# A long convolution and a state-space layer on one core: real and imaginary rows interleaved, the exchange in two strided transfers, a new order

## The chip, the cores and the metric

The kernel runs on one core of one Trainium2 chip. The metric is the device time of an execution in microseconds (us). A core has five engines, each with its own instruction queue: TensorE (PE in the profile, with weight loads shown as PEld), VectorE (DVE), ScalarE (ACT), GpSimd (POOL) and SyncE (SP). In this kernel SP and POOL mostly issue DMA transfers, which 16 DMA engines carry out.

## The reference

Two layers are computed over sequences of 2048 steps and 1024 channels in bf16, and their outputs are put side by side.

```python
# A: shifted key times value, long convolution by FFT, gate
for t in range(ks):
    k_shift = k_shift + k_pad[:, t:t + S, :] * shift_k[:, ks - 1 - t]
kv = k_shift * v
y = irfft(rfft(kv, 2 * S) * rfft(ssm_k, 2 * S))[:S]      # length 4096
A = q * (y + kv * ssm_D)
# B: diagonal complex recurrence
Lam_bar = exp(exp(log_dt) * Lam)
Bu = einsum("bld,pd->blp", x, ((Lam_bar - 1) / Lam)[:, None] * Bmat)
for t in range(L):
    h = Lam_bar * h + Bu[:, t]
B = 2 * einsum("blp,dp->bld", h, Cmat).real + x * Dskip
out = concatenate([A, B], axis=-1)
```

## The kernel before

The whole program is one text, `ORDER`, of some 1500 words. Each word names a task and its arguments; after a colon it names the buffers that the task takes: units of a shared SBUF arena of 53 units of 1024 bf16 columns (a), PSUM banks (p, eight), buffers of the recurrence (h, three) and buffers for transform weights (w, three). The words are executed in order at build time, and every engine's queue receives its instructions in that order; semaphores make an instruction wait for its operands and for the last readers of the buffer it overwrites. `ORDER` therefore sets both the order on each engine and which older buffer each task has to wait for. No planner stands behind it.

**The recurrence (B)** goes in 16 chunks of 128 steps. For a chunk the input is loaded transposed (x), then come four U tasks of two halves each (TensorE, 16 matmuls a half, L435), the copies out of PSUM (ue, ScalarE, L437), a product with a rotation table and a sum (r1 and r2, VectorE, L450 and L457), the carry (cy, ScalarE, L459), two scans (sc, VectorE, L463), a second product and sum (r3, r4, L450 and L469), the output matmuls (y, TensorE, four tasks of four matmuls L479 and one matmul for the skip term L482 for each half of the channels), the copy (ye, L488) and the store (yst, POOL, L490).

**The convolution (A)** does a transform of length 4096 in two stages, 128 by 32. Stage 1 makes kv on VectorE (L514 to L529), transforms it and the filter (am L534, hm L572), copies (ae L540, he L578) and stores to the DRAM tensors Ys_kv and Ys_h (ast L543, hst L581). Stage 2 is the part that the change edits. It runs over 16 pairs of groups. For pair i:

- lw.i loads the pair's transform weights into one of three wslots (SP, L585), lh.i and lk.i load the two stage-1 results (SP, L590);
- sh and sk, one each per group (group 2i and 2i+1), do the 32-point transforms of filter and kv: four matmuls each (L602) whose weights lie in columns 0 to 63 of the group's part of the wslot;
- she copies the filter's spectrum from PSUM to half t=0 of the tile hab, ske that of kv to x16 (ScalarE, L612 and L620);
- sw.i fills half t=1 of hab with the same rows, real and imaginary rows exchanged (POOL issues SBUF-to-SBUF transfers, L625);
- pr.i multiplies both halves of hab by x16 (VectorE, L631), which gives all four real products of a complex one;
- sa, one per group, sums them and transforms back: eight matmuls (L643) with the two remaining blocks of weights;
- sae copies (ScalarE, L651) and vst stores to the DRAM tensor Vs (POOL, L654).

Stage 3 loads Vs (vl, L659), transforms (a3, L671), copies (a3e, L678), multiplies by q (qm, VectorE, L680) and stores (ost, POOL).

A wslot is free for the next pair's lw when the last sa of the pair that used it has read it. The pairs do not run in the order of their numbers; in this `ORDER` lw goes 3, 1, 0, 2, 4, 5, 6, 8, 7, 9, 11, 10, 15, 12, 14, 13.

The 128 partitions of hab hold four runs of 32 rows: real parts of one half of the channels, imaginary parts of that half, and the same for the other half of the channels. sw.i.q for q from 0 to 3 therefore moves one run of 32 rows to its neighbour's place:

```python
o = q ^ 1
dma(hab[32*q:32*q+32, 1], hab[32*o:32*o+32, 0])
```

Of the kernel before, what the change touches and what calls it, by code (L numbers as in the profile page):

```python
# [28 lines left out]
WC = 352  # L29
# [3 lines left out]
def a_constants():  # L33
# [39 lines left out]
bl.1.0:a46 bT.1.0:p1 sin2 bc.1.0 x.1:a47 x.0:a26 ld_F U.1.0.0:a24p4 U.1.3.0:p5 bl.2.0:a48 kvb.2:a49 kp.-2 bc.2.1 bc.7.1 kvm.0:a8 bc.3.0 bl.5.1:a50
vp.1:a40 eo stt kva.0 bl.4.1:a51 kvc.2 bl.5.0:a42 U.0.0.0:a44p7 U.0.0.1 kvb.0:a43 U.1.0.1 bT.2.0:p6 U.0.3.0:p1 ue.0.0 U.0.3.1 bc.2.0 gz bl.4.0:a46
U.1.3.1 bT.4.1:p2 bT.5.1:p3 bT.5.0:p0 cl.3.0:a48 bT.4.0:p7 U.0.1.0:p6 ue.0.3 bc.4.1 bc.4.0 bc.5.1 U.0.1.1 bc.5.0 U.1.1.0:p1 z1 U.0.2.0:p2 U.0.2.1
ue.0.2 ue.0.1 r1.0:a36 U.1.2.0:p7 kvc.3 r2.0:h0 vp.0:a32 kvc.1 kvc.0 cl.2.1:a34 sc.0.1 sc.0.0 cT.2.1:p3 cc.2.1 x.2:a35 z2 cl.1.1:a51 cl.3.1:a50
hl.2:a28 cl.1.0:a42 U.1.2.1 U.2.0.0:a30p0 U.2.0.1 ue.2.0 U.2.1.0:p2 U.2.1.1 ue.2.1 cT.1.1:p6 cc.1.1 U.1.1.1 ue.1.0 ue.1.1 ue.1.2 ue.1.3 r1.1:a8
cT.1.0:p3 r3.0:a0 cc.1.0 r2.1:h1 cT.3.0:p0 cc.3.0 x.3:a46 r4.0 cx.4.1 am.0.1:p2p6 ae.0.1.1:a44 ae.0.0.1 cx.7.0 cl.0.1:a34 am.1.0:p4p1 ae.1.1.0:a40
U.2.3.0:p7 ae.1.0.0 U.2.3.1 ue.2.3 ld_sd:a51 am.0.0:p5p3 ae.0.0.0 U.3.0.0:a32p0 hl.0:a4 U.3.2.0:p6 ae.0.1.0 U.3.0.1 ue.3.0 am.1.1:p2p1 U.2.2.0:p4
hl.3:a6 ae.1.0.1 hl.1:a36 hT.0.0:p7 hc.0.0:a48 hd.0 cy.1 sc.1.0 sc.1.1 ae.1.1.1 U.2.2.1 ue.2.2 r1.2:a8 r3.1:a0 cT.3.1:p5 hT.0.3:p3 cc.3.1 r2.2:h2 r4.1  # L80
# [666 lines left out]
```

## Time and profile before

| | us |
|---|---|
| device time, median of 3 runs | 374.81 |
| the three runs | 372.85, 374.81, 376.28 |
| the profiled execution | 376.32 |
| span of the profiled execution | 374.5 |
| PE busy | 339.6 (91%) |
| PEld busy | 227.5 (61%) |
| DVE busy | 316.8 (85%) |
| ACT busy | 282.6 (75%) |
| POOL busy | 97.7 (26%) |

The granted TensorE clock is 0.983 of full speed on average. The transfers move 101.14 MB at a mean of 270 GB/s; 58.47 MB are issued on the hardware queue (SP) and 42.09 MB on the software queue (POOL).

A share of busy time is a mean over stages that have different limits. The head (weights, tables, first chunks), the middle with stage 1 and the recurrence, the part with stage 2 and the tail have to be read one by one. In a group's row, "idle before" is time in which the engine waited ahead of that instruction, and the name behind it is what ended most of that wait. A line number is that of the printed code.

### The profile page before, as it was taken

Reading aid. Unit: us, or ns where it says so; the run is one execution under the profiler, and the core shown is the slowest. Engines: PE = TensorE matmul, PEld = TensorE weight load, DVE = VectorE, ACT = ScalarE, POOL = GpSimd, SP = SyncE. Lnnn points to the kernel's source line nnn. Section 1 sums busy time; section 2 is a strip of 40 time slices with the busy share of each in tenths; the row PEclk is TensorE's granted clock in tenths of the full one; section 3 lists DMA queues with packets and bytes.
Section 4 is the critical chain, followed back from the end, with each engine's and each line's share of the span. In section 5 each row is a group of like instructions: output and inputs, shape, how many; then the busy total and the mean of one; then the engine's idle time right before and its main releaser. Section 6 shows DMA issues by size and latency. Waiting matters only on the chain.

```text
span 374.5 us, 9087 instructions
## 1 busy us (share of the span) xinstructions
PE 339.6 (91%) x3721; PEld 227.5 (61%) x3721; DVE 316.8 (85%) x249; ACT 282.6 (75%) x538; POOL 97.7 (26%) x167
## 2 busy tenths in 40 slices
PE   4597999999999999999988999697979969999990
PEld 1597997546768895665554495263745746665440
DVE  5998999999999999999969793988764767985970
ACT  4899987946769999986666689696979967327570
POOL 5000000313232232450430415251532431200231
PEclk9999999999999999999998999999999989999996
DMA  6999999486896999998799899989997999798973
GB/s 194 328 313 266 274 333 148 125 297 151 264 314 245 248 315 242 280 284 329 228 290 294 294 218 239 355 256 296 308 270 240 276 313 301 273 329 283 349 302 137
DMA packets 61989, 101.14 MB, mean 270 GB/s; under 512 B 29902, under 2 KB 31966, under 8 KB 61948
## 3 DMA queue, kind: packets, MB, share of 16 engines
q1 hardware_dynamic: 49148, 58.47, 55.7%
q0 software_dynamic: 12800, 42.09, 34.2%
q8 instruction: 29, 0.48, 0.5%
q14 instruction: 12, 0.10, 0.1%
HBM read 52.31 MB, written 33.55 MB: 229 GB/s over the span
## 4 chain that ended last, share of the span: by engine, by line
PE 65%; DMA 14%; ACT 7%; DVE 5%; issue 4%; POOL 2%; POOLq 0%; DVEq 0%; ACTq 0%
PE bank L479 22%; PE bank L435 22%; DMA wslot<-a_c_W 9%; DMA arena<-arena 4%; PE bank L643 4%; PE bank L534 4%; PE bank L572 4%; PE bank L671 3%; PE bank L602 3%; PE bank L556 2%; ACT BT L411 2%; DVE arena L514 2%; ACT arena L612 1%; PE bank L482 1%; DVE arena L631 1%
## 5 line engine op out<-in xcount | busy, mean ns | idle before, releaser
L435 PEld LDWEIGHTS <-BT 128*128 128x128 bf16 x2048 | 118.2, 98 | 14.8 <-issue 6.5
L435 PE MATMUL bank<-arena,BT 128*128 128x128 bf16 x2048 | 125.4, 220 | 1.2 <-ACT BT L411 0.7
L479 PE MATMUL bank<-CT,gslot 128*128 128x512 bf16 x512 | 123.5, 379 | 0.4 <-ACT arena L612 0.2
L479 PEld LDWEIGHTS <-gslot 128*128 128x128 bf16 x512 | 45.6, 98 | 50.5 <-issue 5.4
L463 DVE TENSOR_TENSOR_SCAN gslot<-rtab,gslot 128x1040 bf16<-128x1040 f32 x32 | 73.1, 2312 | 1.8 <-ACT gslot L459 1.5
L631 DVE TENSOR_TENSOR arena<-arena 128x4096 bf16<-128x4096 bf16 x16 | 36.6, 2290 | 24.1 <-DMA arena<-arena 20.7
L625 POOL DMA_DIRECT2D arena<-arena x64 | 31.4, 497 | 62.8 <-ACT arena L612 36.0
L450 DVE TENSOR_TENSOR arena<-arena,Z 128x4096 bf16<-128x4096 bf16 x16 | 36.5, 2284 | 12.6 <-ACT arena L437 12.6
L437 ACT CAST arena<-bank 128x512 bf16<-128x512 f32 x64 | 39.5, 640 | 10.0 <-PE bank L435 6.9
L540 ACT CAST arena<-bank 128x512 bf16<-128x512 f32 x64 | 36.9, 649 | 7.1 <-PE bank L534 6.8
L612 ACT CAST arena<-bank 128x512 bf16<-128x512 f32 x64 | 34.3, 633 | 8.4 <-PE bank L602 8.4
L578 ACT CAST arena<-bank 128x512 bf16<-128x512 f32 x64 | 36.4, 694 | 4.5 <-PE bank L572 2.3
L620 ACT CAST arena<-bank 128x512 bf16<-128x512 f32 x64 | 36.4, 661 | 2.8 <-PE bank L602 2.8
L651 ACT CAST arena<-bank 128x512 bf16<-128x512 f32 x64 | 35.0, 652 | 4.2 <-PE bank L643 3.9
L450 DVE TENSOR_TENSOR arena<-gslot,Z 128x4096 bf16<-128x4096 bf16 x16 | 36.6, 2289 | 0.7
L581 POOL DMA_DIRECT2D Ys_h<-arena x32 | 23.0, 724 | 49.5 <-ACT arena L578 45.1
L488 ACT CAST arena<-bank 128x512 bf16<-128x512 f32 x32 | 19.1, 609 | 19.7 <-PE bank L482 15.6
L514 DVE TENSOR_TENSOR arena<-arena 128x4096 bf16<-128x4096 bf16 (+3 forms) x16 | 30.0, 1883 | 0.5 <-ACT arena L388 0.5
L678 ACT CAST arena<-bank 128x512 bf16<-128x512 f32 x32 | 17.1, 612 | 17.6 <-PE bank L671 17.6
L602 PE MATMUL bank<-arena,wslot 64*64 64x512 bf16 x256 | 20.7, 402 | 9.0 <-DMA wslot<-a_c_W 9.0
L482 PE MATMUL bank<-Dd,arena 128*128 128x128 bf16 x128 | 28.0, 219 | 0.0
L643 PE MATMUL bank<-arena,wslot 64*64 64x512 bf16 x256 | 18.3, 409 | 5.5 <-DVE arena L631 5.3
(96 smaller groups left out, 374.0 us busy)
## 6 DMA issues: line engine op xcount, KB each, us to landing
Ys_kv<-arena POOLq DMA_DIRECT2D x16, 512.0 KB, 5.3
Ys_h<-arena POOLq DMA_DIRECT2D x32, 256.0 KB, 3.8
arena<-Ys_h SPq DMA_DIRECT2D x16, 512.0 KB, 7.8
arena<-Ys_kv SPq DMA_DIRECT2D x16, 512.0 KB, 7.3
arena<-arena POOLq DMA_DIRECT2D x64, 128.0 KB, 6.6
Vs<-arena POOLq DMA_DIRECT2D x16, 512.0 KB, 5.6
arena<-Vs SPq DMA_DIRECT2D x16, 512.0 KB, 8.9
arena<-in_A_k_dram SPq DMA_DIRECT2D x8, 512.0 KB, 5.6
```

Source lines behind the costliest of these rows:

```text
L435: nc.tensor.matmul(pu[:, w, jl, :], BT[:, 2 * jp + jl, w, d, :], xT[:, d, :], start=(d == 0), stop=(d == ND - 1))
L437: E["ue"] = lambda i, jp: nc.scalar.copy(st["u", i][:, :, 2 * jp:2 * jp + 2, :], st.pop(("pu", i, jp)))
L450: nc.vector.tensor_mul(m, s_, win(Z))
L463: nc.vector.tensor_tensor_scan(gf, rtab[:].rearrange("p j t -> p (j t)"), gf, 0.0, ALU.mult, ALU.add)
L479: nc.tensor.matmul(py, h[:, w, j, 2:GW], CT[:, j, w, dh * 512:(dh + 1) * 512], start=(j == 0 and w == 0), stop=False)
L514: nc.vector.tensor_mul(m[:, 0:h0, :], kring_[:, s0:s0 + h0, :], wbc_[:, 0:h0, :])
L540: nc.scalar.copy(st["ysb", n2][:, p, dh * 512:(dh + 1) * 512], st.pop(("pa", n2, p, dh)))
L578: nc.scalar.copy(st["yh", hf, s][:, p, e, :], st.pop(("pb", hf, s, e, p)))
L612: nc.scalar.copy(st["hab", i][:, t, a, l, :], st.pop(("ps", nm, g, l)))
L620: nc.scalar.copy(st["x16", i][:, a, l, :], st.pop(("ps", "k", g, l)))
L631: nc.vector.tensor_mul(hab, st.pop(("x16", i)).rearrange("p a l d -> p (a l d)").unsqueeze(1).to_broadcast([P, 2, 2 * D]), hab)
L651: nc.scalar.copy(st["vsb", i][:, a, dh * 512:(dh + 1) * 512], st.pop(("pv", g, dh)))
```

## The change

The rows of the 32-point transform are ordered anew: instead of 32 real rows and then 32 imaginary rows, real and imaginary rows alternate. This takes a transposition of the constant weights, in the forward blocks and in the two backward blocks that read the product. The exchange of real and imaginary rows is then one of even and odd partitions, so one transfer moves all 64 even rows of the 128 partitions to the odd ones, and a second does the reverse. Per pair there are two issues of 64 rows (256 KB each) where there were four of 32 (128 KB each): 32 issues in all for 64. Each row's data is as long as before.

Each group's weights also lose 32 columns (64 to 95) that no task of the order read, so a pair's load falls from 176 to 160 KB.

`ORDER` is wholly new: nearly every word stands at another place and takes other buffers. Except for the exchange, each kind of task occurs as often as before. In stage 2, lw keeps its order of pairs.

```diff
-WC = 352
+WC = 320
...
-            W[l, :, g, 0:64] = fw.reshape(64, 64)
-            W[l, :, g, 64:96] = fw[:, :, 0, :].reshape(64, 32)
+            W[l, :, g, 0:64] = fw.transpose(0, 1, 3, 2).reshape(64, 64)
...
-                W[dh, :, g, 96 + 128 * l:160 + 128 * l] = wa.reshape(64, 64)
-                W[dh, :, g, 160 + 128 * l:224 + 128 * l] = wb.reshape(64, 64)
+                W[dh, :, g, 64 + 128 * l:128 + 128 * l] = wa.transpose(1, 0, 2, 3).reshape(64, 64)
+                W[dh, :, g, 128 + 128 * l:192 + 128 * l] = wb.transpose(1, 0, 2, 3).reshape(64, 64)
...
-lw.9:w2 sh.18:p2p7 sw.7.1 sh.19:p6p4 sw.7.0 sa.17:p1p3
+lw.9:w2 sh.19:p2p1 yst.8 ske.15.0 lh.11:a20 ye.10.1:a27 sae.16.0:a50
...
     def swap(dma, i, q):
-        o = q ^ 1
-        dma(st["hab", i][32 * q:32 * q + 32, 1, :, :, :], st["hab", i][32 * o:32 * o + 32, 0, :, :, :])
+        dma(st["hab", i][q:P:2, 1, :, :, :], st["hab", i][1 - q:P:2, 0, :, :, :])
...
-                    c0 = a * WC + 96 + 128 * l + 64 * t
+                    c0 = a * WC + 64 + 128 * l + 64 * t
```

Line numbers of the code after the change are three to seven lower than those of before. The next rows show the order of instructions on an engine, with line, operation, output and input, and in brackets the semaphores waited for: DMASW and DMAHW count landings of transfers issued by POOL and by SP, eight counters each; the others count an engine's instructions.

On POOL, one pair's exchange (pair 9) between two stores of Vs, before:

```order
L625 DMA arena<-arena 32x2048 [waits DVE_49,DMASW1_49,PE_49,Activation_49]
L625 DMA arena<-arena 32x2048 [waits DMASW2_49,PE_49]
L625 DMA arena<-arena 32x2048 [waits DMASW3_49]
L625 DMA arena<-arena 32x2048 [waits DMASW4_49]
L654 DMA Vs<-arena 128x2x1024 [waits DMAHW2_49,DMASW5_49,Activation_49]
```

An exchange after, with the stores of Vs around it:

```order
L647 DMA Vs<-arena 128x2x1024 [waits DMAHW0_49,DMASW4_49,Activation_49]
L618 DMA arena<-arena 64x2048 [waits DVE_49,DMASW5_49,PE_49,Activation_49]
L618 DMA arena<-arena 64x2048 [waits DMASW6_49]
L647 DMA Vs<-arena 128x2x1024 [waits DMASW7_49]
L647 DMA Vs<-arena 128x2x1024 [waits DMASW0_49,Activation_49]
```

Four issues have become two. Each of POOL's issues still waits for the landing counter of the one eight issues before it.

On ScalarE, the copies ahead of the first copy (L612, after L607) that belongs to pair 9, whose first sh stands behind the reload of a wslot that pair 6 used. Before:

```order
376 L651 CAST arena_91<-bank7_99 128x512
377 L651 CAST arena_91<-bank6_98 128x512
378 L620 CAST arena_91<-bank4_96 128x512
379 L620 CAST arena_91<-bank1_93 128x512
380 L620 CAST arena_91<-bank3_95 128x512
381 L620 CAST arena_91<-bank0_92 128x512
382 L488 CAST arena_91<-bank5_97 128x512
383 L612 CAST arena_91<-bank7_99 128x512
```

After:

```order
374 L644 CAST arena_91<-bank4_96 128x512
375 L614 CAST arena_91<-bank0_92 128x512
376 L614 CAST arena_91<-bank6_98 128x512
377 L614 CAST arena_91<-bank3_95 128x512
378 L614 CAST arena_91<-bank5_97 128x512
379 L614 CAST arena_91<-bank2_94 128x512
380 L434 CAST arena_91<-bank1_93 128x2x256
381 L614 CAST arena_91<-bank7_99 128x512
382 L485 CAST arena_91<-bank4_96 128x512
383 L644 CAST arena_91<-bank0_92 128x512
384 L607 CAST arena_91<-bank7_99 128x512
```

Between the last copy of pair 6's back transform (the first row of the second piece) and the first copy of pair 9 there now also stand two more copies of kv's spectrum (L614), one of a U task (L434) and one of pair 8's back transform (L644), so the TensorE work that they read lies inside this reload too.

On VectorE, the products (L631, after L624) of the last three pairs, 12, 14 and 13, with the first product of chunk 13 (L450, after L447, with the table Z1). Before:

```order
214 L631 TENSOR_TENSOR arena_91<-arena_91 128x4096 [waits DMASW6_49,DMASW1_49,DMASW7_49,DMASW0_49,Activation_49]
215 L450 TENSOR_TENSOR arena_91<-arena_91,Z1_74 128x4096 [waits DMAHW6_49,Activation_49]
216 L631 TENSOR_TENSOR arena_91<-arena_91 128x4096 [waits DMASW5_49,DMASW4_49,DMAHW0_49,DMASW3_49,DMAHW3_49,DMASW2_49,Activation_49]
217 L457 TENSOR_TENSOR gslot0_85<-arena_91 128x16x128 [waits DVE_49]
218 L631 TENSOR_TENSOR arena_91<-arena_91 128x4096 [waits DMASW2_49,DMASW7_49,DMASW1_49,DMAHW2_49,DMASW0_49,Activation_49]
219 L463 SCALAR_TENSOR_TENSOR gslot0_85<-rtab_76,gslot0_85 128x1040 [waits DVE_49,Activation_49]
```

After:

```order
211 L624 TENSOR_TENSOR arena_91<-arena_91 128x4096 [waits DMASW6_49,DMAHW7_49,DMASW5_49,Activation_49]
212 L624 TENSOR_TENSOR arena_91<-arena_91 128x4096 [waits DMASW1_49,DMASW0_49,Activation_49]
213 L624 TENSOR_TENSOR arena_91<-arena_91 128x4096 [waits DMAHW1_49,DMAHW2_49,DMASW3_49,DMAHW4_49,DMASW2_49,Activation_49]
214 L447 TENSOR_TENSOR arena_91<-arena_91,Z1_74 128x4096 [waits DMAHW3_49,PE_49]
215 L454 TENSOR_TENSOR gslot0_85<-arena_91 128x16x128 [waits DVE_49]
216 L460 SCALAR_TENSOR_TENSOR gslot0_85<-rtab_76,gslot0_85 128x1040 [waits DVE_49,Activation_49]
```

The first product and sum of chunk 13, which stood between the last three pairs' products, now stand behind them. In the same place on TensorE the U tasks of the last two chunks stand ahead of the remaining y tasks of chunk 12.

More of the change, by code (lines that the diff above doesn't have):

```diff
@@ L73 @@
[L73 to L80, printed above, removed]
@@ new lines @@
+U.3.3.0:p4 he.0.0.0.1 he.0.0.0.0 hc.0.5:a20 U.3.3.1 cT.2.1:p7 hc.0.2:a36 cc.2.1 ae.0.1.1 ast.0 cx.6.1 vp.2:a24 U.3.2.0:p0 hm.0.5.1:p6p2 U.3.2.1
+he.0.5.1.0:a28 he.0.5.1.1 cx.5.0 ue.3.2 cy.2 sc.2.1 sc.2.0 kvb.4:a27 kva.6 r3.2:a0 kvb.6:a40 r4.2 y.0.0.0:p1 y.0.0.1 ue.3.3 hm.0.2.0:p7p3 hT.0.3:p6
+hc.0.3:a52 r1.3:a16 y.0.0.2 y.0.0.3 ye.0.0:a21 hm.0.5.0:p2p0 kvc.4 he.0.5.0.0 he.0.5.0.1 hT.0.4:p4 hc.0.4:a20 he.0.2.0.1:a38 y.1.0.0:p6 hm.0.2.1:p1p2
+y.1.0.1 he.0.2.0.0 he.0.2.1.0 hst.0.2.0 hT.0.1:p0 hc.0.6:a36 hT.0.7:p4 hm.0.4.1:p3p7 he.0.4.1.1:a22 cx.4.1 y.1.0.2 y.1.0.3 ye.1.0:a30 he.0.4.1.0
@@ new lines @@
+am.2.0:p1p5 ae.2.0.0:a32 cx.5.1 hst.0.0.0 cx.7.0 hst.0.5.1 y.1.1.0:p7 y.1.1.1 y.1.1.2 hm.0.6.1:p6p3 hc.0.7:a31 am.2.1:p1p4 ae.2.0.1 ae.2.1.1 y.1.1.3
+r2.3:h1 kvm.5:a0 kp.4 ye.1.1 he.0.2.1.1 kvm.9:a16 kva.5 kva.9 kvb.5:a41 ae.2.1.0 cy.3 sc.3.0 kvb.9:a47 sc.3.1 vp.3:a34 kvm.8:a0 r3.3:a16 ld_G
+he.0.6.1.1:a50 kva.8 r4.3 he.0.6.1.0 kvc.6 y.0.1.0:p1 kvb.8:a16 y.0.1.1 ast.1 kvc.5 kvm.7:a0 hc.0.1:a42 hst.0.0.1 vp.4:a44 kvc.8 x.4:a43 kva.7
+kvb.7:a17 hm.0.4.0:p4p7 y.0.1.2 y.0.1.3 ye.0.1 kvc.9 y.2.0.0:p2 hst.0.2.1 y.2.0.1 y.2.0.2 y.2.1.0:p5 y.2.1.1 he.0.4.0.0 y.2.1.2 am.4.0:p3p6
@@ new lines @@
+ae.4.0.0:a38 ae.4.1.0 y.2.1.3 am.4.1:p0p1 ye.2.1:a20 ae.4.0.1 hm.0.6.0:p4p3 he.0.6.0.0 ae.4.1.1 y.2.0.3 ast.2 ye.2.0 yst.1 hm.0.7.1:p6p5
+he.0.7.1.1:a32 he.0.4.0.1 hst.0.6.0 hm.0.7.0:p0p4 yst.0 he.0.7.0.0 hst.0.5.0 U.4.0.0:a36p1 he.0.6.0.1 he.0.7.1.0 hst.0.7.0 he.0.7.0.1 U.4.0.1
+am.3.0:p2p5 ae.3.0.0:a30 U.4.1.0:p7 U.4.2.0:p0 U.4.3.0:p3 U.4.1.1 ue.4.1 ue.4.0 U.4.3.1 U.4.2.1 kp.5 ue.4.3 ae.3.1.0 ue.4.2 r1.4:a0 r2.4:h0 lw.3:w0
+kvc.7 kvm.11:a0 kva.11 kvb.11:a48 am.3.1:p6p4 ae.3.1.1 x.5:a27 U.5.0.0:a28p2 U.5.3.0:p7 U.5.3.1 ae.3.0.1 U.5.1.0:p1 kvm.10:a0 U.5.0.1 kva.10
@@ new lines @@
+ast.3 kp.6 hl.6:a30 hT.1.0:p1 hc.1.0:a16 hd.1 r3.4:a0 vp.5:a40 kvc.11 r4.4 kvc.10 ast.5 am.7.0:p6p0 kp.7 kvm.15:a0 kva.15 ae.7.0.0:a24 kvb.15:a49
+kvm.13:a0 kva.13 am.7.1:p2p7 ae.7.1.1 kvb.13:a17 x.6:a47 ae.7.1.0 vp.7:a28 kvc.15 ae.7.0.1 hst.0.3.0 hst.0.7.1 kvm.12:a0 kva.12 kvb.12:a46
+U.8.0.0:a32p4 U.8.0.1 ue.8.0 vp.6:a40 kvc.13 ast.8 ast.9 hm.0.1.1:p3p5 hst.0.3.1 hT.1.1:p1 hc.1.1:a44 hT.1.7:p6 U.8.2.0:p7 hm.0.1.0:p0p2 hc.1.7:a45
+he.0.1.0.0:a36 U.8.3.0:p4 kvc.12 he.0.1.1.0 he.0.1.0.1 hm.1.7.0:p1p6 kvm.14:a0 hT.1.2:p0 U.8.3.1 he.1.7.0.0:a18 ast.7 hst.0.1.0 he.1.7.0.1 ue.8.3
@@ new lines @@
+U.6.2.0:p7 he.1.4.0.0 U.6.2.1 y.4.0.0:p2 ue.6.2 ue.6.1 r1.6:a8 hst.1.1.1 r4.5 ae.11.1.1 r2.6:h1 hm.1.4.1:p0p1 he.1.4.1.0 y.4.0.1 he.1.4.1.1 y.4.0.2
+y.4.0.3 ye.4.0:a16 hm.1.6.0:p4p3 yst.3 he.1.6.0.1:a34 x.13:a18 hm.1.2.0:p7p5 hst.1.1.0 he.1.2.0.1:a44 hm.1.6.1:p6p0 he.1.6.0.0 he.1.2.0.0 he.1.6.1.0
+ast.11 he.1.6.1.1 hst.1.0.0 hst.1.4.0 y.4.1.0:p1 hm.1.2.1:p2p3 x.7:a19 hm.1.3.1:p5p4 he.1.3.1.0:a50 x.11:a48 x.10:a52 y.4.1.1 x.9:a23 he.1.2.1.1
+he.1.3.1.1 hm.1.3.0:p7p6 hst.1.0.1 y.4.1.2 lw.0:w2 he.1.2.1.0 am.13.1:p0p5 ae.13.1.1:a40 he.1.3.0.1 y.4.1.3 ye.4.1 hm.1.5.1:p3p4 am.10.0:p2p5
@@ new lines @@
+ske.4.1 lw.4:w1 ske.5.1 sh.4:p7p6 y.8.0.0:p3 y.8.0.1 y.8.0.2 y.8.0.3 she.5.1:a8 ske.5.0 she.4.0 lh.7:a20 she.5.0 sh.8:p2p5 sw.3.0 sw.3.1 pr.3 she.4.1
+sa.7:p1p0 sh.9:p7p4 ye.8.0:a22 sae.7.0:a2 sa.6:p6p3 she.9.0:a40 lk.7:a36 U.10.0.0:a38p1 she.8.1 she.9.1 U.10.0.1 ue.10.0 y.8.1.0:p7 y.8.1.1
+U.10.3.0:p5 U.10.3.1 vst.1 y.8.1.2 y.8.1.3 sae.7.1 sae.6.1 r1.9:a32 r2.9:h1 sae.6.0 she.8.0 cy.9 sw.2.1 lk.6:a4 x.14:a49 ue.10.3 ye.8.1 lw.5:w0
+sh.11:p4p1 sh.10:p0p3 she.11.0:a12 she.11.1 sw.2.0 pr.2 sa.5:p6p2 sa.4:p5p7 sae.4.0:a24 U.11.0.0:a6p4 U.11.0.1 she.10.1 U.10.2.0:p1 U.10.2.1 she.10.0
@@ new lines @@
+sc.11.0 sw.9.1 ske.23.0:a42 U.12.1.0:p7 she.23.1 r3.11:a12 she.22.0 U.12.1.1 r4.11 lh.15:a6 she.22.1 lw.10:w0 ue.12.0 ske.23.1 ue.12.1 sh.21:p2p0
+she.21.0:a8 sh.20:p3p6 she.21.1 she.20.1 she.20.0 sw.9.0 pr.9 sk.21:p1p4 ske.21.0:a46 ske.21.1 U.12.2.0:p5 vst.7 U.12.2.1 ue.12.2 yst.9 vst.8
+sa.18:p7p2 sae.18.1:a4 sa.19:p0p6 sae.19.1 r1.12:a12 sae.18.0 sk.20:p3p1 r2.12:h1 ske.20.1 ske.20.0 sae.19.0 qp.0:a16 sk.22:p4p5 y.11.1.0:p2 y.11.1.1
+y.11.1.2 y.11.1.3 lk.12:a20 lw.15:w2 sh.30:p6p7 ske.22.1 ske.22.0 she.30.0:a32 sk.31:p1p3 sh.31:p0p5 she.31.1 she.30.1 ye.11.1:a52 U.13.0.0:a40p4
@@ L165 @@
+y.15.1.2 ost.4 y.15.1.3 ye.15.0:a28 ye.15.1 yst.15
 """
@@ L592, in full_kernel, with s2 @@
     E["lk"] = lambda i: l2("k", Ys_kv, i)
-    def s2(nm, g, c0=0):
+    def s2(nm, g):
         i, a = divmod(g, 2)
-        pk = "j" if c0 else nm
         for l in range(2):
-            st["ps", pk, g, l] = bank()
+            st["ps", nm, g, l] = bank()
         for dh in range(2):
@@ L601, in s2 @@
                 rows = slice(64 * l, 64 * l + 64)
-                nc.tensor.matmul(st["ps", pk, g, l][64 * dh:64 * dh + 64, :], st["w", i][rows, a * WC + c0:a * WC + c0 + 64],
+                nc.tensor.matmul(st["ps", nm, g, l][64 * dh:64 * dh + 64, :], st["w", i][rows, a * WC:a * WC + 64],
                                  st[nm, i][rows, a, dh * 512:(dh + 1) * 512], start=True, stop=True)
```

161 lines of the change are left out of this document (68 added, 93 removed).

## The prediction

> **What bounds the kernel now.** I read the busy time by stretch first, then the waits of the stretch that loses most, then the chain of work there. The columns of the first view are the stretch, its length, the busy time of PE, PEld, DVE, ACT and POOL with instruction counts, the granted clock, the DMA share and GB/s.
>
> ```profile
> 0.00:60.00 60.00, 48.77 (x723) 43.48 (x724) 53.67 (x85) 52.34 (x84) 6.73 (x16) 1.00 1.01 278
> 60.00:180.00 120.00, 119.84 (x1200) 80.94 (x1198) 119.08 (x90) 96.13 (x184) 35.48 (x52) 1.00 0.83 248
> 180.00:317.00 137.00, 122.08 (x1462) 76.26 (x1460) 104.71 (x53) 108.21 (x220) 46.12 (x86) 0.98 0.97 281
> 317.00:357.50 40.50, 40.50 (x301) 22.86 (x299) 34.29 (x20) 20.35 (x42) 4.69 (x7) 1.00 0.90 313
> 357.50:374.50 17.00, 8.39 (x45) 3.91 (x43) 5.06 (x5) 5.54 (x11) 4.68 (x7) 0.82 0.53 204
> ```
>
> TensorE is the bound from 60 to 180 us and from 317 to 357 us: it idles 0.2 us of 120 and none of 40.5. It loses 11.2 us in the head, 8.6 us at the end, and 14.9 us (137.00 less 122.08) between 180 and 317 us. That last stretch holds the second transform stage with the exchange that the change touches. Its waits (engine, line, what it waited for: us in total, times, longest):
>
> ```profile
> POOL arena L625 <- ACT arena L612: 36.0, 9, 13.8
> DVE arena L631 <- DMA arena<-arena: 20.7, 8, 4.3
> PEld L602 <- DMA wslot<-a_c_W: 10.6, 6, 3.1
> PE bank L643 <- DVE arena L631: 5.3, 2, 2.8
> ```
>
> Two causes cover the 14.9 us. In six places the next pair's first matmuls (L602) wait for their weights, since the slot was free only when an older pair's last L643 had ended. In two places L643 waits for the product on VectorE (L631), which had waited for the exchange. VectorE's 20.7 us matter only through those 5.3 us. The chain in order of time (start, us, what) shows both:
>
> ```profile
> 185.88 9.32 DMA arena<-arena
> ...
> 195.42 2.30 DVE arena L631
> ...
> 226.69 7.07 DMA arena<-arena
> ...
> 236.32 1.09 PE bank L643 x16
> ...
> 237.42 4.67 DMA wslot<-a_c_W
> ...
> 242.14 0.44 PE bank L602 x4
> ...
> 250.16 6.31 DMA wslot<-a_c_W
> ...
> 256.52 0.63 PE bank L602 x8
> 257.14 0.86 PE bank L643 x16
> ...
> 263.28 5.98 DMA wslot<-a_c_W
> ...
> 269.30 1.00 PE bank L602 x12
> ...
> 274.36 6.65 DMA wslot<-a_c_W
> ...
> 281.05 1.06 PE bank L602 x16
> ...
> 286.10 3.99 DMA wslot<-a_c_W
> ...
> 290.13 1.06 PE bank L602 x16
> ...
> 297.27 6.52 DMA wslot<-a_c_W
> ...
> 303.83 1.92 PE bank L602 x16
> ```
>
> **The reload term.** From the end of the last L643 on a slot to the first L602 on the new weights the six places take 4.72, 6.36, 6.02, 6.69, 4.03 and 6.56 us (start of the L602 row less start of the DMA row). In the program's order these are the loads for pairs 8, 9, 10, 15, 12 and 13. TensorE fills part of that time with other work, which the order lists. Prices of that work:
>
> ```profile
> 330.87 0.89 PE bank L435 x16
> 331.77 0.86 PE bank L479 x4
> 332.63 0.06 PE bank L482
> ```
>
> So one U task (16 matmuls L435) is 0.89 us, one y task (L479 x4, L482) 0.92, one sa (8 of L643; x16 took 0.86) 0.43, one sh or sk (4 of L602; x16 took 1.06) 0.27. The cover before: pair 8, 3 y + 2 sa = 3.62; pair 9, 4 y + 1 sk = 3.95; pair 10, 5 U + 3 sh/sk = 5.26; pair 15, 4 y + 1 sk = 3.95; pair 12, 2 sa + 2 U + 1 y = 3.56; pair 13, 4 U = 3.56. The uncovered parts are 1.10, 2.41, 0.76, 2.74, 0.47 and 3.00, together 10.5 us, which is the 10.6 us of the wait row. The method reproduces the profile, so I apply it to the new order: pair 8, 3.62 again; pair 9, 2 U + 4 y + 3 sk + 2 sa = 7.13; pair 10, 6 U + 3 sh/sk = 6.15; pair 15, 4 y + 2 sk = 4.22; pair 12, 1 sk + 1 U + 2 sa + 2 y = 3.86; pair 13, 4 U + 4 sh/sk = 4.64. Uncovered: 1.10, 0, 0, 2.47, 0.17, 1.92 = 5.7 us. The term is **-4.8 us**. The cover for pairs 9 and 10 is TensorE work; if sa of pair 8, which is now inside pair 9's cover, is itself held by its product, that cover is gone and 2.4 us come back. Of the other seven reloads pairs 5, 6, 7, 11 and 14 have at least 6.1 us of cover, pair 4 has 8.3 (12 before) and pair 2 the same y and sa work as before; none had a wait. Bounds: 0 and -10.5.
>
> **The exchange term.** Per pair four POOL issues of 32 rows become two of 64; bytes stay at 512 KB.
>
> ```profile
> L625 POOL DMA_DIRECT2D arena<-arena x64: 489/492/528, 179.8 to 308.3; - x64
> DMA to landing us min/median/max: 2.3/6.6/10.3
> Ys_h<-arena POOLq DMA_DIRECT2D x32, 256.0 KB, 3.8
> ...
> POOL arena L625 <- DMA arena<-arena: 3.7, 3, 1.5
> ...
> L581 POOL DMA_DIRECT2D Ys_h<-arena x32 | 23.0, 724 | 49.5 <-ACT arena L578 45.1
> ```
>
> An issue of 64 rows has no row. Below it stand the 32-row issue at 0.49 us, above it the 256-row one at 0.72; I take 0.55. Two cost 1.1 us for 2.0, so the last half leaves 0.9 us sooner. POOL then saves about 14 us in all, hidden: it is busy 46.1 of 137 us there and waits 36 us for ScalarE's copies. Behind each waiting issue stand only the next exchange and POOL's stores of Vs and of the outputs. Each POOL issue also waits for the landing of the one eight before it; that wait (below) falls with half the issues, and is as hidden. Landing of a 256 KB half lies between 2.3 us (the fastest 128 KB half) and 13.2 us (twice the median). I take the 6.6 us of today, because the four halves of a pair are in flight together and their last one brings the same 512 KB. On the path lie only the two places that sum to 5.3 us, pairs 0 and 5. There the shorter issue gives 2 x 0.9 = 1.8 us. The order also puts more TensorE work between their last sh and first sa, by the prices above: 16.7 us against 12.5, and 14.7 against 12.0. Against that, pairs 14, 15 and 6 get less: 11.4 for 15.9, 10.0 for 12.6 and 12.5 for 14.2. I take **-2.5 us**, between -5.3 and, with landing at the upper end, +9.
>
> [...]
>
> **Small terms.** The weights shrink from 176 to 160 KB.
>
> ```profile
> wslot<-a_c_W SPq DMA_DIRECT2D x16, 176.0 KB, 5.7
> ```
>
> Were all of a load's 5.7 us proportional to size, four uncovered loads would gain 4 x 0.5 = 2 us; fixed cost alone gives 0. I take -0.3, near fixed cost, since 128 KB has landed in 2.3 and in 10.3 us. The granted clock of 0.98 over 137 us costs 2.7 us and is low beside the waits; with half of them gone I take -0.7 (0 to -2.7). In the head the order has 4.25 MB of loads ahead of the first U task for 4.75, but ScalarE has the same 16 weight copies, tables and evictions ahead of the last one that the first rotation needs; I take 0 (-2 to +2).
>
> In the tail VectorE has one rotation's products and sum and one more gating product after the last pair: 2.3 + 1.2 + 1.2 = 4.7 us more.
>
> ```profile
> 341.05 2.29 DVE L450 TENSOR_TENSOR arena<-arena,Z 128x4096 bf16<-128x4096 bf16 x1 [5.11 <-ACT arena L437]
> 343.45 1.23 DVE L457 TENSOR_TENSOR gslot<-arena 128x2048 bf16<-128x2048 bf16 x1
> 344.59 1.22 DVE L680 TENSOR_TENSOR arena<-arena 128x2048 bf16<-128x2048 bf16 x1
> ```
>
> It idled 5.1 us there for the evictions of the last U tasks. The new order puts those before the last y tasks of chunk 12, so that idle covers the 4.7. I take 0. TensorE too has 2.7 us more work between the last pair's first sa and the last chunk's first y (43.8 for 41.1, by the prices above, with 0.43 for the two matmuls L671 of an a3 task from the row below); without the cover it is therefore +2.0.
>
> ```profile
> 336.69 0.43 PE bank L671 x2
> ```
>
> **New waits** of an order made anew are the least known term. Like stretches lost 0.2 us (60 to 180) and 14.9 us (180 to 317). I take +2.3, a sixth of the upper one, as no counted cover but pair 4's got shorter and that one stays long.
>
> **Sum:** -4.8 - 2.5 - 0.3 - 0.7 + 0 + 0 + 2.3 = -6.0 us. Against the profiled span of 374.5 that is 368.5. The profiled execution took 376.32 us, 1.5 above the median of the three runs; from the median 374.81 the forecast is **368.8 us**.
>
> **The rivals.** (1) *The gain is given back to the transfers.* The stretch runs at a DMA share of 0.97 and moves the same bytes but 256 KB. If its pace is the transfers', a load that is asked for sooner lands no sooner. For it: landings near 6 us everywhere. Against it: TensorE's waits sum exactly from cover and latency, and pair 12's load came in 4.03 us. Then nothing is left but 1 us of issue: 374 us. (2) *The larger halves land later, and it is slower.* One half carries twice the rows; if its landing exceeds 6.6 us, pairs 13, 15, 8 and 14, with 9.7 to 11.4 us of cover, pay directly, since issue, landing, product and copies take about 12 us. At +3 us that is 12 us, and with the 6 us gained 381 us. It decides from +1.5 us (break-even, 8.1 us of landing); beyond 9.0 us it is slower by over 1%. For it: the maximum of 10.3. Against it: 256 KB to HBM land in 3.8. (3) *The tail becomes VectorE's* (+2.0) with pair 9's cover lost (+2.4): 373.2 us.
>
> **How the numbers follow.** Within about 1% (371.1 to 378.6 us) a measurement of this kernel can't be told from no change. Forecast 0.56, its own range 363.5 to 371; rival 1 0.22; rival 3 0.06; rival 2 0.16. The range for 8 in 10 reaches over the forecast and rivals 1 and 3: 363.5 to 377; it leaves out rival 2 and some 0.03 below. Faster 0.56, same 0.28 (rivals 1 and 3), slower 0.16.
>
> **What would show each step.** Reloads: L602's wait for the weights at 5 to 7 us and no such row for pairs 9 and 10. Exchange: 32 issues near 0.55 us, median landing at or below 6.6 us, L643's wait for L631 under 3 us. Clock: above 0.98 in this stretch. Tail: no TensorE gap before the last chunk's y tasks. Rival 1 shows as longer landings of the weights with the same waits; rival 2 as landings above 8 us. The forecast is wrong if TensorE waits in this stretch for something that has no row today.

## The result and the profile after

The changed kernel takes 362.94 us (median of 4 runs, 362.16 to 365.9) against 375.45 us for the kernel before (median of 4, 372.85 to 376.28). The ratio is 0.9693, with a 95% interval from 0.9618 to 0.9768: faster by 3.1%, which is 12.5 us by the medians. The forecast was 368.8 us with a range from 363.5 to 377. The sign was right, the gain was twice the 6.0 us forecast, and the median lies 0.6 us under the range. Some executions came out 1 to 3% longer at a lower granted clock (in two_blocks_same_side 376.17 us at 0.976, against 369.96 at 0.988): the medians hold them, the ratios leave them out, and the traces shown below of four_strided_halves and two_blocks_same_side are of such executions.

The busy time of the changed kernel by stretch, with the columns as before the change (length, busy time and instructions of PE, PEld, DVE, ACT and POOL, granted clock, DMA share, GB/s). The third stretch ends with the last back transform of stage 2, as the third one before did:

```profile
0.00:60.00 60.00, 49.43 (x742) 44.70 (x744) 53.96 (x85) 54.01 (x88) 5.43 (x14) 1.00 0.98 272
60.00:180.00 120.00, 119.44 (x1202) 81.32 (x1211) 119.28 (x91) 96.40 (x185) 38.69 (x56) 1.00 0.86 259
180.00:302.50 122.50, 116.69 (x1384) 72.31 (x1396) 100.36 (x50) 105.83 (x216) 30.82 (x51) 0.99 0.93 316
302.50:345.00 42.50, 42.29 (x320) 25.75 (x323) 35.85 (x21) 21.06 (x43) 5.27 (x8) 0.96 0.81 286
345.00:361.80 16.80, 9.61 (x52) 4.49 (x50) 6.15 (x6) 5.08 (x10) 4.02 (x6) 0.87 0.43 159
```

Stage 2 ends 14.5 us sooner (302.5 for 317.0 us), and 1.8 us of that come back behind it (59.3 for 57.5 us), because the order has more work of the last chunks there. TensorE's idle time in the third stretch fell from 14.9 to at most 5.8 us; at most, since the trace lacks records of 28 matmuls (3693 for 3721 weight loads), about twelve of them in this stretch by its row. The same stretch's waits, changed kernel:

```profile
DVE arena L624 <- DMA arena<-arena: 6.0, 2, 5.5
...
PEld L636 <- DVE arena L624: 4.9, 5, 2.2
...
PE bank L636 <- ACT arena L644: 1.7, 1, 1.7
...
PE bank L636 <- DVE arena L624: 1.5, 2, 1.3
```

No row for the weights is left: the 10.6 us that the weight loads of L602 waited for them are gone, not the 4.8 us forecast. Counted by the matmuls instead, that wait was 9.0 us before:

```profile
PE bank L602 <- DMA wslot<-a_c_W: 9.0, 6, 2.9
```

The wait for the product fell less than the row of 1.5 us says. The 1.7 us that the matmuls seem to wait for a copy of ScalarE (L644) stand at 300.48 us, and there the weight loads of the same task, which start 0.01 us ahead of the matmuls, had waited for the product, which ended at 300.42 (start, us, what, and in brackets the idle time ahead and what ended it):

```profile
298.13 2.29 DVE L624 TENSOR_TENSOR arena<-arena 128x4096 bf16<-128x4096 bf16 x1 [0.45 <-DMA arena<-arena]
```

```profile
297.73 0.58 PEld L636 LDWEIGHTS <-wslot 64*64 64x64 bf16 x16 [1.64 <-DVE arena L624]
300.47 0.19 PEld L636 LDWEIGHTS <-wslot 64*64 64x64 bf16 x8 [2.17 <-DVE arena L624]
```

So the matmuls lost about 3.2 us to the product (1.5 and 1.7), against 5.3 before. They lost them at pairs 14 and 13, and no longer at pairs 0 and 5.

What shortened the waits shows in the transfers, first more of the kernel before (POOL's queue with packets, MB and its share of 16 engines' time; an issue's size and median us to landing), then the changed kernel:

```profile
q0 software_dynamic: 12800, 42.09, 34.2%
...
arena<-Ys_kv SPq DMA_DIRECT2D x16, 512.0 KB, 7.3
```

```profile
q0 software_dynamic: 12288, 42.09, 31.6%
...
arena<-arena POOLq DMA_DIRECT2D x32, 256.0 KB, 4.5
arena<-Ys_kv SPq DMA_DIRECT2D x16, 512.0 KB, 5.4
...
wslot<-a_c_W SPq DMA_DIRECT2D x16, 160.0 KB, 3.3
```

An exchange issue carries twice the bytes and lands in 4.5 instead of 6.6 us. The loads of weights, which the change touches by a tenth of their size, land in 3.3 instead of 5.7 us, and those of the stage-1 result Ys_kv, which it does not touch, in 5.4 instead of 7.3. POOL's queue moves the same 42.09 MB in 114.3 us of each engine's time for 128.1 (31.6% of 361.8 against 34.2% of 374.5). So POOL's transfers took 13.8 us less of each engine's time for the same bytes, and loads that the change hardly touches gained too.

### The profile page after: what moved, and what is told of

The parts are those of the page before. It is cut to its first block, busy times and chain, and to the rows that moved or that the text cites. A ratio compares the mean times of both kernels' runs of the same rounds, so it can differ in the third digit from the quotient of the medians.

```text
span 361.8 us, 8974 instructions
## 1 busy us (share of the span) xinstructions
PE 337.5 (93%) x3693; PEld 228.6 (63%) x3721; DVE 315.6 (87%) x249; ACT 282.4 (78%) x538; POOL 84.2 (23%) x135
## 3 DMA queue, kind: packets, MB, share of 16 engines
q0 software_dynamic: 12288, 42.09, 31.6%
## 5 line engine op out<-in xcount | busy, mean ns | idle before, releaser
L432 PEld LDWEIGHTS <-BT 128*128 128x128 bf16 x2048 | 118.9, 99 | 12.2 <-issue 7.1
L476 PE MATMUL bank<-CT,gslot 128*128 128x512 bf16 x488 | 120.9, 379 | 2.4 <-DVE gslot L466 0.8
L434 ACT CAST arena<-bank 128x512 bf16<-128x512 f32 x64 | 40.3, 659 | 13.1 <-PE bank L432 12.9
L624 DVE TENSOR_TENSOR arena<-arena 128x4096 bf16<-128x4096 bf16 x16 | 36.3, 2286 | 14.8 <-DMA arena<-arena 6.0
L447 DVE TENSOR_TENSOR arena<-arena,Z 128x4096 bf16<-128x4096 bf16 x16 | 36.5, 2282 | 6.3 <-ACT arena L434 6.1
L644 ACT CAST arena<-bank 128x512 bf16<-128x512 f32 x64 | 35.7, 660 | 4.7 <-PE bank L636 4.7
L614 ACT CAST arena<-bank 128x512 bf16<-128x512 f32 x64 | 37.1, 688 | 0.3 <-PE bank L598 0.3
L447 DVE TENSOR_TENSOR arena<-gslot,Z 128x4096 bf16<-128x4096 bf16 x16 | 36.6, 2288 | 0.6
L607 ACT CAST arena<-bank 128x512 bf16<-128x512 f32 x64 | 35.6, 691 | 1.1 <-PE bank L598 1.1
L578 POOL DMA_DIRECT2D Ys_h<-arena x32 | 23.8, 762 | 34.0 <-ACT arena L575 33.9
L618 POOL DMA_DIRECT2D arena<-arena x32 | 17.5, 548 | 45.0 <-ACT arena L607 29.4
L540 POOL DMA_DIRECT2D Ys_kv<-arena x16 | 11.3, 707 | 71.4 <-ACT arena L537 59.9
L647 POOL DMA_DIRECT2D Vs<-arena x16 | 11.8, 738 | 53.9 <-ACT arena L644 50.6
```

The source lines that it names most:

```text
L432: nc.tensor.matmul(pu[:, w, jl, :], BT[:, 2 * jp + jl, w, d, :], xT[:, d, :], start=(d == 0), stop=(d == ND - 1))
L434: E["ue"] = lambda i, jp: nc.scalar.copy(st["u", i][:, :, 2 * jp:2 * jp + 2, :], st.pop(("pu", i, jp)))
L447: nc.vector.tensor_mul(m, s_, win(Z))
L476: nc.tensor.matmul(py, h[:, w, j, 2:GW], CT[:, j, w, dh * 512:(dh + 1) * 512], start=(j == 0 and w == 0), stop=False)
L607: nc.scalar.copy(st["hab", i][:, 0, a, l, :], st.pop(("ps", "h", g, l)))
L614: nc.scalar.copy(st["x16", i][:, a, l, :], st.pop(("ps", "k", g, l)))
```

## Experiments

Three things change at once: which rows one issue takes, how many issues there are, and the order. The runs change them one at a time. Each time stands beside runs of the kernel before on the same chip.

| run | order | issues per pair | rows of one issue | us (median) | ratio to before, interval |
|---|---|---|---|---|---|
| strided_four_old_order | old | 4 x 32 | every 4th of 128 | 365.05 | 0.9707, 0.9605 to 0.9809 |
| two_strided_old_order | old | 2 x 64 | every 2nd of 128 | 364.68 | 0.9651, 0.9576 to 0.9726 |
| old_exchange_new_order | new | 4 x 32 | 32 neighbours | 375.41 | 1.0006, 0.9960 to 1.0051 |
| two_blocks_of_64 | new | 2 x 64 | 64 neighbours, read from the other half | 370.81 | 0.9826, 0.9751 to 0.9901 |
| two_blocks_same_side | new | 2 x 64 | 64 neighbours, read from the same half | 373.60 | 0.9881, 0.9809 to 0.9954 |
| four_strided_whole | new | 4 x 32 | every 4th of 128 | 366.20 | 0.9683, 0.9616 to 0.9751 |
| four_strided_halves | new | 4 x 32 | every 2nd of one half of 64 | 375.54 | 1.0035, 0.9956 to 1.0114 |
| weights_of_352_columns | new | 2 x 64 | every 2nd of 128 | 363.93 | 0.9615, 0.9547 to 0.9684 |
| exchange_on_SyncE | new | 2 x 64, by SP | every 2nd of 128 | 363.54 | 0.9607, 0.9527 to 0.9686 |
| new_order_again | new | 2 x 64 | every 2nd of 128 | 363.21 | 0.9643, 0.9599 to 0.9686 |
| old_order_again | old | 2 x 64 | every 2nd of 128 | 364.87 | 0.9683, 0.9641 to 0.9725 |

**Only the rows of an issue, in the kernel before** (strided_four_old_order). The weights' rows are interleaved as in the change; order, number of issues and size of the weights are those of before.

```diff
         o = q ^ 1
-        dma(st["hab", i][32 * q:32 * q + 32, 1, :, :, :], st["hab", i][32 * o:32 * o + 32, 0, :, :, :])
+        dma(st["hab", i][q:P:4, 1, :, :, :], st["hab", i][o:P:4, 0, :, :, :])
```

> The kernel before, its order and its four issues of 32 rows per pair; only the rows are interleaved, so that each issue takes every fourth partition. Theory 1 (pattern): transfers between runs of 32 neighbouring partitions are slow and hold up the others, strided ones are not. The weights then land in about 3.3 us as after the change, the exchange near 4.5; the reload waits fall from 10.6 to about 1 us, the exchange's from 5.3 to 1-3: 362 to 367 us. Theory 2 (order): the new order made the gain: no change, 374 to 377 us. Theory 3 (fewer, larger issues): no change, 374 to 377 us.

365.05 us: nearly the whole gain, with nothing moved. Its waits in stage 2, and its loads of weights:

```profile
PEld L643 <- DVE arena L631: 3.6, 4, 1.6
...
PEld L602 <- DMA wslot<-a_c_W: 2.2, 4, 0.8
...
PE bank L643 <- DVE arena L631: 1.1, 1, 1.1
...
PE bank L602 <- DMA wslot<-a_c_W: 1.1, 2, 0.6
```

```profile
arena<-arena POOLq DMA_DIRECT2D x64, 128.0 KB, 4.7
...
wslot<-a_c_W SPq DMA_DIRECT2D x16, 176.0 KB, 4.3
```

With 176 KB as before, the weights land in 4.3 instead of 5.7 us, and the wait for them falls from 10.6 to 2.2 us in the old order. Both fell less than expected (3.3 and about 1 us). Not every load gained: those of Ys_h took 7.7 us for 7.8. The weights' own packets explain little of it: their 1408-byte packets that began between 176 and 300 us, by the packet records' own clock, took 83 ns on average before and 74 ns here. A load has 128 of them on 16 engines, so this makes less than 0.1 us of the 1.4 (an estimate). More likely the loads waited less behind other transfers, but no run shows that directly. The theory of the order and the theory of fewer issues both said 374 to 377 us, and both fall as main causes.

**Two issues as well, order of before** (two_strided_old_order): the code of the change under the old order, of whose four exchange words per pair the first two stay.

```diff
-sw.9.0 sw.9.1 sw.9.2 sw.9.3 pr.9
+sw.9.0 sw.9.1 pr.9
```

> The code after the change with the order of before (its first two exchange words of a pair kept). Theory 1 (pattern): 361 to 367 us, no wait on the weights above 1 us in sum. Theory 2 (order): the reload waits of 10.6 us stay, exchange 0.9 us sooner at two places: 372 to 375 us. Theory 3 (fewer, larger issues): 361 to 367 us.

364.68 us. Its weight loads still waited 3.2 us for the weights, more than the 1 us expected. Going from four strided issues to two, with the smaller weights, gained 0.4 us in the old order, which no interval here can tell from nothing.

**The new order with the exchange of before** (old_exchange_new_order). The rows are as before, each exchange word issues two of the four blocks, the weights keep 160 KB.

```diff
-        dma(st["hab", i][q:P:2, 1, :, :, :], st["hab", i][1 - q:P:2, 0, :, :, :])
+        for r in (2 * q, 2 * q + 1):
+            o = r ^ 1
+            dma(st["hab", i][32 * r:32 * r + 32, 1, :, :, :], st["hab", i][32 * o:32 * o + 32, 0, :, :, :])
```

> The kernel after the change with the rows of before and four issues of 32 neighbouring partitions per pair, in the new order. Theory 1 (pattern) and theory 3 (fewer, larger issues): the weights land in 5 to 6 us again, the new order's covers leave about 5.7 us uncovered, the exchange costs 2 to 3 more: 369 to 373 us. Theory 2 (order): 362 to 365 us.

375.41 us: no gain at all, more than either theory had said. Its waits in stage 2:

```profile
PEld L638 <- DVE arena L626: 13.5, 6, 6.4
DVE arena L626 <- DMA arena<-arena: 12.3, 6, 7.9
...
PE bank L638 <- DVE arena L626: 10.4, 4, 6.1
...
PEld L598 <- DMA wslot<-a_c_W: 5.3, 4, 1.7
```

The wait for the weights is halved, to 5.3 us. The prediction's count of cover had said 5.7, but the sums agree partly by luck. By place the waits are 1.24 us at pair 8 (1.10 counted), 0.71 at pair 15 (2.47), 1.75 at pair 13 (1.92), and 1.65 at pair 2, which the count had taken as covered. The median landing here was 4.7 us, not the 5 to 6 expected.

The time did not follow: what was gained there went into the wait for the product. The rows in which the last pairs lose it, first on POOL, then on VectorE, then TensorE's weight loads:

```profile
290.42 1.94 POOL L620 DMA_DIRECT2D arena<-arena  x4 [2.68 <-ACT arena L607]
293.50 1.45 POOL L620 DMA_DIRECT2D arena<-arena  x3 [1.13 <-ACT arena L607]
299.52 0.49 POOL L620 DMA_DIRECT2D arena<-arena  x1 [4.57 <-DMA arena<-arena]
```

```profile
304.16 2.29 DVE L626 TENSOR_TENSOR arena<-arena 128x4096 bf16<-128x4096 bf16 x1 [7.87 <-DMA arena<-arena]
309.11 2.29 DVE L626 TENSOR_TENSOR arena<-arena 128x4096 bf16<-128x4096 bf16 x1 [2.66 <-ACT arena L646]
```

```profile
306.50 0.19 PEld L638 LDWEIGHTS <-wslot 64*64 64x64 bf16 x8 [6.42 <-DVE arena L626]
311.45 0.19 PEld L638 LDWEIGHTS <-wslot 64*64 64x64 bf16 x8 [3.91 <-DVE arena L626]
```

The new order puts the exchanges of pairs 14 and 13 close behind each other at the end. By the records of the trace, pair 14's four issues (the first row) land 10.2 to 12.2 us after their issue. VectorE's 7.87 us are the wait for the last of them, and TensorE's weight loads pay 6.42 us.

The last of pair 13's four waits 4.57 us on POOL. The row names an exchange, but the semaphore that came last there is that of the store of Vs eight issues before, which had taken 12 us to land (issued at 286.99, landed at 299.24). Pair 13's last issue then lands at 308.72, after pair 14's product is done; the product of pair 13 follows at 309.11, and TensorE pays 3.91 us. The row's copy of ScalarE ends only at that moment and isn't what it waited for.

In the changed kernel the same two places cost 1.64 and 2.17 us (above): pair 14's two issues land 6.5 and 7.4 us after their issue, and none waits on POOL for a landing. The new order by itself is worth nothing here.

**Two issues of 64 neighbours** (two_blocks_of_64): number and size of the issues as in the change, other rows.

```diff
-        dma(st["hab", i][q:P:2, 1, :, :, :], st["hab", i][1 - q:P:2, 0, :, :, :])
+        o = 1 - q
+        dma(st["hab", i][64 * q:64 * q + 64, 1, :, :, :], st["hab", i][64 * o:64 * o + 64, 0, :, :, :])
```

> The kernel after the change, order and two issues of 64 rows kept, but each issue moves 64 neighbouring partitions to the other 64 instead of every second one. This leaves the exchange of the right rows out, with as many bytes. Theory 1 (pattern): as slow as the old exchange, weights landing in 5 to 6 us, 368 to 373 us. Theories 2 and 3 (order; fewer, larger issues): 362 to 365 us.

370.81 us, in the range for the pattern and outside that for fewer, larger issues. One part of the pattern's theory failed: the weights landed in 4.5 us, not in 5 to 6, and the matmuls waited only 0.9 us for them. What this run loses is the wait for the product, 10.4 us. It is still 4.6 us better than four blocks of 32.

**Neighbours, or one half of the partitions?** The next two differ in one thing: which rows go together into one issue. Both have four issues of 32 rows, and in both no two rows of an issue are neighbours.

The first, four_strided_whole:

```diff
-        dma(st["hab", i][q:P:2, 1, :, :, :], st["hab", i][1 - q:P:2, 0, :, :, :])
+        for r in (2 * q, 2 * q + 1):
+            o = r ^ 1
+            dma(st["hab", i][r:P:4, 1, :, :, :], st["hab", i][o:P:4, 0, :, :, :])
```

> The kernel after the change, order kept, with four issues per pair instead of two, each of 32 rows taken as every fourth of all 128 partitions. Theory 4 (sides: an issue is slow whose rows lie in one half of 64 partitions) and theory 5 (neighbours: an issue is slow whose rows are next to each other): 362 to 366 us, the exchange landing in 4 to 5 us. Theory 3 (fewer, larger issues): slower by the 4.6 us that lie between two blocks of 64 and four of 32, 366 to 370 us.

The second, four_strided_halves:

```diff
-        dma(st["hab", i][q:P:2, 1, :, :, :], st["hab", i][1 - q:P:2, 0, :, :, :])
+        for h in range(2):
+            dma(st["hab", i][64 * h + q:64 * h + 64:2, 1, :, :, :], st["hab", i][64 * h + 1 - q:64 * h + 64:2, 0, :, :, :])
```

> As the run before, four issues of 32 rows, but each takes every second row of one half of 64 partitions. The only difference between the two is which rows go into one issue. Theory 4 (sides): slow as with blocks, 369 to 377 us, L636's waits for the product above 8 us in sum. Theory 5 (neighbours): 362 to 366 us.

366.20 and 375.54 us, with intervals far apart. The first lies 0.2 us above the range of theories 4 and 5 and at the lower end of that of theory 3, so the number of issues has a part too (below). The waits in stage 2, first of the issues over all partitions, then of those over one half each:

```profile
PE bank L638 <- DVE arena L626: 4.4, 3, 2.3
```

```profile
PEld L637 <- DVE arena L625: 15.6, 5, 6.6
...
PE bank L637 <- DVE arena L625: 12.2, 4, 6.2
```

Rows two apart in one half of 64 are as slow as 32 neighbours in the same order (375.54 and 375.41 us). So it is not nearness: the changed order with the rows of an issue in one half of the partitions took 370.81 to 375.54 us in these runs, with rows of both halves 362.94 to 366.20. No run takes neighbours from both halves (partitions 32 to 95, say), so it isn't shown whether lying on both sides of the middle is enough. The slow run's weights landed in 3.8 us, and the weight loads waited 0.3 us for them: this run loses its time to the product alone, while old_exchange_new_order also lost some to the weights.

On the same chip the two strided issues with the larger weights (weights_of_352_columns, below) took 363.93 us, 2.3 us less than four, and every run of the one was shorter than every run of the other. So in the new order the number of issues has a part that did not show in the old one (0.4 us there). The wait of pair 13's last issue for the store eight issues before fits a part of this. It returns here, shorter, and the matmuls wait 4.4 us for the product where the changed kernel has 3.2:

```profile
293.86 0.53 POOL L620 DMA_DIRECT2D arena<-arena  x1 [1.77 <-DMA Vs<-arena]
```

The packets show the difference one step nearer. These are the transfer times of the 4 KB packets of POOL's queue that began between 176 and 300 us, taken from the packet records of each trace (by their own clock, which starts 10.5 us ahead of the span in the traces of before and after); about half of them belong to the exchange, the rest to stores:

```
run                        packets  mean ns  median  90th percentile  over 250 ns
before                        3810    220.4     168              314        27.7%
old_exchange_new_order        4052    211.1     160              320        24.5%
two_blocks_of_64              4080    215.4     160              321        31.0%
two_blocks_same_side          3945    215.7     160              331        30.0%
four_strided_halves           4022    203.2     160              311        19.3%
strided_four_old_order        4170    174.7     159              179         3.8%
two_strided_old_order         4050    176.6     159              184         5.4%
four_strided_whole            4101    171.9     159              186         4.6%
after                         4121    173.9     159              196         5.8%
```

Wherever an issue's rows lie in one half, 19 to 31% of the packets take more than 250 ns, and the 90th percentile stands near 320 ns, twice the median of 159 to 160 ns of the kernels with rows over all partitions. In those under 6% do. Why packets of one half take longer, no run shows. The share of slow packets does not order the slow kernels among themselves: four_strided_halves has the smallest and, at 375.54 us, the longest time.

**Reads and writes on one side** (two_blocks_same_side):

```diff
-        dma(st["hab", i][q:P:2, 1, :, :, :], st["hab", i][1 - q:P:2, 0, :, :, :])
+        dma(st["hab", i][64 * q:64 * q + 64, 1, :, :, :], st["hab", i][64 * q:64 * q + 64, 0, :, :, :])
```

> The kernel after the change with two issues of 64 neighbouring rows, each copied within its own half of the partitions (the exchange of the right rows is left out). In the earlier run with two blocks of 64 each issue read one half and wrote the other: 370.8 us. If reading and writing the same side is what costs: slower than that, 372 to 378 us. If one side for the reads and one for the writes is enough to cost it: the same, 369 to 372 us.

373.60 us (369.96 to 376.17) against 370.81: the two ran on different chips, the intervals of their ratios overlap, and the packets are alike. Whether reading and writing one half is worse than reading one and writing the other stays open.

**The smaller weights** (weights_of_352_columns):

```diff
-WC = 320
+WC = 352
```

> The kernel after the change with the 32 unused columns of weights per group put back (176 KB a load, not 160). The strided exchange explains the sooner landing: weights in 3.3 to 4 us, 362 to 365 us. If the smaller load explains it: landing above 5 us, reload waits of 4 us or more, 366 to 370 us.

363.93 us, and 176 KB land in a median of 3.6 us for 3.3. The size of the load is not what made the weights land sooner; it is worth 1 us at most by the medians, which the intervals do not tell from nothing.

**The exchange issued by SyncE** (exchange_on_SyncE):

```diff
-    E["sw"] = lambda i, q: swap(gpd, i, q)
+    E["sw"] = lambda i, q: swap(spd, i, q)
```

> The kernel after the change with the exchange issued by SyncE instead of GpSimd. If what counts is which rows an issue takes: the exchange lands as now or sooner and TensorE's waits stay; but each exchange waits for ScalarE's copies and SyncE's loads of weights and of stage-1 results stand behind it, so 364 to 378 us. If GpSimd's issue (0.55 us) and its queue held the exchange: 358 to 362 us.

363.54 us, the same within the intervals and 0.5 us under the range of the first answer. TensorE's waits did not stay: those of the matmuls for the product fell from 3.2 to about 2.3 us, and those for the weights, whose loads now stand behind the exchange, came back with 2.8 us. The time can't tell whether GpSimd's queue alone cost anything; a move to SyncE gains nothing.

**What the order is worth** (new_order_again, which is the changed kernel itself, and old_order_again, which repeats two_strided_old_order):

> The kernel after the change once more, beside the next run on the same chip. If the new order by itself is worth nothing: the same as the next run within 1 us, about 364 us. If it is worth the 1.8 us that lay between 364.68 and 362.94: 361 to 363 us.

> The code after the change with the order of before, two strided issues per pair. If the new order by itself is worth nothing: within 1 us of the run before, about 364 us. If it is worth 1.8 us: 364 to 366 us.

363.21 and 364.87 us: 1.7 us, as the first comparison had 1.7 (362.94 and 364.68). The two ratios' intervals overlap, so 1.7 us is the likely size and not a proven one. No variant beat the changed kernel.

## Why the prediction was right in sign and half the size

*The step that failed* is the latency in the reload term: it took the 4.0 to 6.7 us of before for the new order too. Behind it stands an assumption of the exchange term: "I take the 6.6 us of today, because the four halves of a pair are in flight together and their last one brings the same 512 KB". The same bytes did not cost the same: with the exchange's rows in both halves the 4 KB packets of POOL's queue took 173.9 ns on average, with 32 neighbours 220.4 before the change and 211.1 in the new order. No row of before shows an exchange of other rows than 32 neighbours, and the sum has no term for the choice of rows. What a cheaper exchange does for the loads of weights was not priced at all.

*Reloads.* The term was -4.8 us and became -10.6 (-9.0 counted by the matmuls). The prediction had added this row of weight loads to a row of matmuls, 10.6 and 5.3, which is more than the 14.9 us that it explains; by matmuls alone it is 14.3. Three of the four places that the count left uncovered did show a wait under the old exchange; pair 12 showed none, and the sum of 5.3 us for 5.7 needed the 1.65 us of pair 2. The latency that the count held fixed fell with the landing (5.7 to 3.3 us in the median; 4.7 with the old exchange in the new order). The strided rows alone left 2.2 us of the wait, the order alone 5.3, both together none. And without the faster exchange this term was worth nothing in time (375.41 us, a ratio of 1.0006): what the order's cover gained there went into the wait for the product.

*Exchange.* The issue was taken at 0.55 us:

```profile
L618 POOL DMA_DIRECT2D arena<-arena x32: 519/544/567, 176.2 to 290.3; - x32
...
DMA to landing us min/median/max: 2.2/4.5/8.5
```

It is 0.544 us. The landing is 4.5 us for the 6.6 taken, and the matmuls' wait for the product fell by 2.1 us (5.3 to 3.2) for the 2.5 taken. That this is near is partly luck: the waits at pairs 0 and 5 went, as the prediction had it, but new ones came at pairs 14 and 13. It had named pair 14 as losing cover, and gave no price for it. The prediction called the landing counter of the issue eight before "as hidden"; with four blocks in the new order it was not (4.57 us on POOL, above); with two strided issues POOL has no such wait.

*New waits.* TensorE's idle places in stage 2 and behind it that the trace gives a cause to, changed kernel:

```profile
201.25 1.04 PE L476 MATMUL bank<-CT,gslot 128*128 128x512 bf16 x4 [0.78 <-DVE gslot L466]
...
261.92 1.06 PE L636 MATMUL bank<-arena,wslot 64*64 64x512 bf16 x16 [0.17 <-DVE arena L624]
275.14 0.81 PE L476 MATMUL bank<-CT,gslot 128*128 128x512 bf16 x3 [0.16 <-issue]
...
297.73 1.06 PE L636 MATMUL bank<-arena,wslot 64*64 64x512 bf16 x16 [1.30 <-DVE arena L624]
300.48 1.92 PE L636 MATMUL bank<-arena,wslot 64*64 64x512 bf16 x16 [1.69 <-ACT arena L644]
```

Those that are neither weights nor product are 0.78 and 0.16, together 0.9 us; +2.3 was taken, a sixth of 14.9 us and so a guess. The 1.69 belongs to the product, as said above. Of the at most 5.8 us of idle time 1.7 have no row. The 0.78 us for VectorE (L466) has no row in the kernel before, which the prediction had named as a sign of being wrong; it is small.

*Weights, clock, head, tail.* Taken at -0.3, -0.7, 0 and 0. The weights' size stayed within what can be measured. The mean clock went from 0.983 to 0.985. The head's idle time went from 11.2 to 10.6 us, that of the last stretch from 8.6 (of 17.0) to 7.2 (of 16.8), and TensorE has no gap before the last y tasks: 0.2 us of 42.5. These are within the bounds given.

*The rivals.* Rival 1 held that the transfers set the pace of the stretch. In that it named what the forecast left out; it erred in taking their cost as a matter of bytes, and its sign, longer landings of the weights, did not show. Rival 2, larger halves that land later, is contradicted by the 4.5 us. What it warned of, too little cover at pairs 13 and 14, is what the new order with four blocks showed. Rival 3 did not occur.

## What to carry to other kernels

A transfer between parts of SBUF that moves fewer than all partitions may gain from rows of both halves of the partitions. Here, with 32 or 64 rows an issue, every second or every fourth of 128 was worth 8 to 12 us of 375 against rows of one half, at equal bytes, issues and order, so a layout that makes this possible is worth a run. Where the transfers keep the DMA engines as full as here (a share of 0.97 in the third stretch before), price a transfer also by what the loads beside it lose, and not only by its own wait: of the 11.1 us that the matmuls waited less for weights and product, 9.0 were waits for loads of weights that hardly changed. An order that covers one wait must be judged with the waits that it uncovers: under the old exchange the new order gained 5.0 us of the matmuls' waits for weights (9.0 to 4.0) and lost 5.1 to the product, at the last two exchanges above all.

## What the hardware did that was not expected

When the rows of an exchange issue lay in one half of the partitions, 19 to 31% of the 4 KB packets on POOL's queue took over 250 ns, with a 90th percentile near 320; with rows over both halves it was 4 to 6%, with a median of 159 ns. Spacing of the rows by two within a half did not help (375.5 us against 366.2). The effect reached the loads of weights, which do not depend on the exchange beside them: in the old order, with nothing changed but the rows, their median landing fell from 5.7 to 4.3 us.
